# Residual codec kernel on one core: row norms and scores from 64-row blocks on two column tiles, the tap sum kept in z, and the schedule retuned

## The chip, the cores and the metric

The kernel runs on one core of one Trainium2 chip. The metric is the device time of one execution in microseconds (us). Each ratio to the kernel before compares fast runs of one chip session. Two other runs that are compared may come from different sessions, on different chips; the kernel before had a median of 781.0 to 781.5 us in all of them, and where the times and the ratios give different sizes, both are said. The program is static: a small planner inside the kernel's source lays out, before anything runs, in which order each engine issues its instructions and which of two engines gets each shareable piece of work.

## The reference, cut to what matters

```
B, T, D, K = 2, 16000, 512, 3          # Nq, C = 4, 8
z = sum over 3 taps of x[t-1..t+1] * dw_enc          # depthwise
z = z * sigmoid(z)                                   # the gate
res = z; q = 0
for s in range(4):                                   # four codebooks of 8 vectors
    d2  = |res|^2 - 2 res.cb[s] + |cb[s]|^2
    sel = cb[s][argmin(d2)]
    q += sel; res -= sel
y = sum over 3 taps of q[t-1..t+1] * dw_dec
```

All arrays are bfloat16, and the choices have to follow the reference's rounding, so the row norm |res|^2 is needed, once for the first three codebooks and once again for the fourth, from the residual.

Of the kernel before, what the change touches and what calls it, by code (L numbers as in the profile page):

```python
# [16 lines left out]
class Plan:  # L17



    AGAIN = {"PE": 0.0, "ACT": 0.1, "DVE": 0.12, "POOL": 0.1, "SP": 0.0}
# [3 lines left out]
    def __init__(self, pairs, share, quota, when):  # L25
        self.steps, self.writer, self.readers = [], {}, {}
        self.pairs, self.share, self.quota, self.when = pairs, share, quota, when

    def add(self, engine, cost, key, fn, reads=(), writes=(), take=None, free=None, hold=None, tail=0.0, after=(), dest=None):
        n = len(self.steps)  # L30
        deps = set(after)
        for t in reads:
            if t in self.writer:
                deps.add(self.writer[t])
            self.readers.setdefault(t, []).append(n)
        for t in writes:
            if t in self.writer:
                deps.add(self.writer[t])
            deps.update(self.readers.get(t, ()))
            self.writer[t] = n  # L40
            self.readers[t] = []
        deps.discard(n)
        self.steps.append({"n": n, "e": engine, "c": cost, "k": key, "fn": fn, "deps": sorted(deps), "take": take, "free": free,
                           "hold": hold, "tail": tail, "dest": dest})
        return n

    def order(self):
# [3 lines left out]
        rank = [self.when[s["k"][0]][0] + s["k"][1] + self.when[s["k"][0]][1] * s["k"][2] for s in steps]  # L51
# [12 lines left out]

        def place(kind, t):
# [4 lines left out]
        def soonest(s, now):  # L70
            t = max(at[s["n"]], now)
            if s["take"]:
                if s["dest"] == "ANY":
                    if all(held[d] >= self.quota[d] for d in self.quota):
                        return inf
                elif s["dest"] and held[s["dest"]] >= self.quota[s["dest"]]:
                    return inf
                t = place(s["take"][0], t)[0]
            return t

        def open_(n):
            if steps[n]["e"]:
                waiting[steps[n]["e"]].append(n)
# [4 lines left out]
        while len(out) < len(steps):  # L88
            t, _, n = min((soonest(steps[n], clock[e]), rank[n], n) for e, names in waiting.items() for n in names)
            assert t < inf  # L90
            s = steps[n]
            e, c = s["e"], s["c"]
            if s["take"]:
                kind, box = s["take"]
                j = place(kind, t)[2]
# [3 lines left out]
                box["dest"] = s["dest"]  # L99
                if s["dest"] == "ANY":  # L100
                    load = {d: max(clock[d] - t, 0.0) + held[d] + sum(steps[m]["c"] for m in waiting[d] if at[m] <= t + 1.0) for d in ("ACT", "DVE")}
                    full = [d for d in load if held[d] >= self.quota[d]]
                    box["dest"] = ("ACT" if full[0] == "DVE" else "DVE") if full else "DVE" if load["DVE"] + self.share[box["part"]] < load["ACT"] else "ACT"
                    c = c[box["dest"]]
                    steps[n + 1]["e"], steps[n + 1]["c"] = box["dest"], steps[n + 1]["c"][box["dest"]]
                if box["dest"]:
                    held[box["dest"]] += 1
# [3 lines left out]
            s["t"], s["d"] = t, c  # L111
# [8 lines left out]
            waiting[e].remove(n)  # L120
            out.append(s)
            for u in users[n]:
                at[u] = max(at[u], t + c + self.AGAIN[e] if steps[u]["e"] == e else end + self.LATENCY[e])
# [8 lines left out]
def kernel(  # L132
# [21 lines left out]
    ZW = P + NC  # L154
    NX, NP, NZ, NOH, NY = 2, 3, 3, 4, 4
    NA = 4
    SHARE = (6.05, 4.21, -1.54)
    QUOTA = {"ACT": 2, "DVE": 4}
    WHEN = {"setup": (0.738, 0), "load": (-2, 1), "pad": (-1.5, 0), "taps": (0.156, 0.45),
            "exp": (-0.071, 0.45), "plus1": (-0.859, 0.482), "recip": (0.56, 0.492), "gate": (0.894, 0.536),  # L160
            "score0": (1.076, 0.045), "decide": (1.235, 0.171), "win0": (2.058, 0), "resid": (1.684, 0.7),
            "score3": (2.362, 0.507), "decide3": (2.6, 0), "win3": (2.763, 0.334), "back": (2.621, 0.723)}
# [11 lines left out]
    for b, sizes in enumerate(SIZES):  # L174
        done = 0
        for g in sizes:
# [4 lines left out]
                          "split": [(q, min(q + 6, g)) for q in range(0, g, 6)]})  # L181
# [12 lines left out]
    MSK = sb([P, 3, ZW], BF16, "MSK")  # L194
# [6 lines left out]
    P0 = [sb([P, 2, GM * P], BF16, f"P0{b}") for b in range(NP)]  # L201
    P1 = [sb([P, 2, GM * P], BF16, f"P1{b}") for b in range(NP)]
    ZB = [sb([P, KT, GM, ZW], BF16, f"ZB{b}") for b in range(NZ)]
# [21 lines left out]
    plan = Plan(NA, SHARE, QUOTA, WHEN)  # L225
# [36 lines left out]
    def setup():  # L262
# [7 lines left out]
        for u in range(3):  # L270
            add("DVE", 0.2, key, lambda u=u: nc.vector.tensor_scalar(out=MSK[:, u, N3:N3 + P], in0=IDENT, scalar1=BIG, scalar2=-BIG,
                op0=ALU.mult, op1=ALU.add), ["I"], ["MSK"])
# [19 lines left out]
        for b in range(NZ):  # L292
            for i in range(KT):
                eng = "ACT" if b == 0 else "DVE"
                f = nc.scalar.copy if b == 0 else nc.vector.tensor_copy
                add(eng, 0.4, ("setup", 0.9 + b, 0), lambda b=b, i=i, f=f: f(ZB[b][:, i, :, 0:N3], CBM2[:, i:i + 1, 0:N3].to_broadcast([P, GM, N3])),
                    [("CBM2", i)], [("ZC", b)])
                add(eng, 0.25, ("setup", 0.9 + b, 0), lambda b=b, i=i, f=f: f(ZB[b][:, i, :, N3 + P:ZW], CBM2[:, i:i + 1, N3:NC].to_broadcast([P, GM, C])),
                    [("CBM2", i)], [("ZC", b)])
# [99 lines left out]
    def front(st, h):  # L399
# [4 lines left out]
        sl = hc % NP  # L404
        p0, p1 = P0[sl][:, :, 0:R], P1[sl][:, :, 0:R]
        allx = [("X", xs, g) for g in range(1, G + 2)] + [("XE", xs)]
        pt = [[("P0", sl, c) for c in range(2)], [("P1", sl, c) for c in range(2)]]

        def tap(dst, i, k):
            return lambda: nc.vector.tensor_scalar(out=dst, in0=X[:, i, k:k + G, :].rearrange("p g c -> p (g c)"),  # L410
                                                   scalar1=WENC[:, k, i:i + 1], scalar2=None, op0=ALU.mult)
        for k in range(K):
            for c in range(2):
                add("DVE", dve(R, 3.84) + 0.06, ("taps", n, h), tap((p1 if k else p0)[:, c], 2 * h + c, k), allx + ["WENC"], [pt[k > 0][c]])
            if k:
                tt(p0, p0, p1, ALU.add, dve(2 * R, 1.92), ("taps", n, h), pt[1], pt[0])
        add("ACT", act(2 * R), ("exp", n, h), lambda: nc.scalar.activation(p1, p0, ACT.Exp, scale=-1.0),  # L417
            [("P0", sl, 0), ("P0", sl, 1)], [("P1", sl, 0), ("P1", sl, 1), "ACTTAB"], hold="E")
        add("DVE", dve(2 * R, 3.84), ("plus1", n, h), lambda: nc.vector.tensor_scalar(out=p1, in0=p1, scalar1=1.0, scalar2=None, op0=ALU.add),
            [], [("P1", sl, 0), ("P1", sl, 1)])  # L420
        return sl, p0, p1

    def front2(st, h, sl, p0, p1):
        n, G = st["n"], st["G"]
        R = G * P
        add("ACT", act(2 * R), ("recip", n, h), lambda: recip(p1, p1), [], [("P1", sl, 0), ("P1", sl, 1), "ACTTAB"], hold="R")
        Z = ZB[n % NZ]
        o = Z[:, 2 * h:2 * h + 2, 0:G, N3:N3 + P]
        tt(o, p0.rearrange("p i (g c) -> p i g c", c=P), p1.rearrange("p i (g c) -> p i g c", c=P), ALU.mult, dve(2 * R, 1.92),
           ("gate", n, h), [("P0", sl, 0), ("P0", sl, 1), ("P1", sl, 0), ("P1", sl, 1)],  # L430
           [("Z", n % NZ, i, u) for i in (2 * h, 2 * h + 1) for u in range(2)])

# [6 lines left out]
    def gram(st, g0, g1, c0, c1, box):  # L439
        Z = ZB[st["n"] % NZ]  # L440
        w = c1 - c0
        pgr = ps(box)
        for b0 in range(g0, g1, 3):
            nb = min(3, g1 - b0)
            o = pgr[:, 512 * ((b0 - g0) // 3):512 * ((b0 - g0) // 3) + nb * w]
            nc.tensor.matmul(o, lhsT=IDENT, rhs=MSK[:, 0:nb, c0:c1], start=True, stop=False)  # L446
            for u in range(nb):
                for i in range(KT):
                    nc.tensor.matmul(o[:, u * w:(u + 1) * w], lhsT=Z[:, i, b0 + u, N3:N3 + P],  # L449
                                     rhs=Z[:, i, b0 + u, c0:c1], start=False, stop=(u == nb - 1 and i == KT - 1))  # L450

    def views(g0, g1, w, box):
        pgr = ps(box)
        if g1 - g0 == 6:
            return [(g0, 6, pgr.rearrange("p (b w) -> p b w", b=2)[:, :, 0:3 * w].rearrange("p b (u w) -> p b u w", w=w))]
        return [(b0, min(3, g1 - b0), pgr[:, 512 * ((b0 - g0) // 3):512 * ((b0 - g0) // 3) + min(3, g1 - b0) * w].rearrange(
            "p (b u w) -> p b u w", b=1, w=w)) for b0 in range(g0, g1, 3)]

    def grp(t, g0, n):
        return t[:, g0:g0 + n, :].rearrange("p (b u) c -> p b u c", b=2 if n == 6 else 1)  # L460

    def gram_cost(g0, g1, w):
# [258 lines left out]
```

## The kernel before: the parts that the change touches

Rows are handled in 18 tiles; 14 of them hold 16 groups of 128 rows, the first two and the last two hold 6 or 8. The 512 channels are four chunks of 128 partitions (`KT = 4`). One tile passes through these stages.

*Front* (VectorE and ScalarE), in two halves `h` of two channel chunks each. The taps are multiplied and added into `P0`, ScalarE takes `exp` into `P1` and later the reciprocal, and VectorE multiplies the two into z (`ZB`, three buffers). z is first written here, at the gate:

```python
# front: p0, p1 are one of three slots each
for k in range(K):
    for c in range(2):
        add("DVE", ..., tap((p1 if k else p0)[:, c], 2 * h + c, k), ...)
    if k:
        tt(p0, p0, p1, ALU.add, ...)
add("ACT", ..., lambda: nc.scalar.activation(p1, p0, ACT.Exp, scale=-1.0), ...)
add("DVE", ..., p1 = p1 + 1)
# front2
add("ACT", ..., lambda: recip(p1, p1), ...)
o = Z[:, 2 * h:2 * h + 2, 0:G, N3:N3 + P]
tt(o, p0..., p1..., ALU.mult, ..., writes=[("Z", n % NZ, i, u) ...])
```

*Scores* (TensorE, then VectorE). Beside each 128-row block of z lie the codebooks' columns times -2, so one matmul of the block with itself gives the scores and, on the diagonal, the row norms. A mask matmul first puts -2^100 off the diagonal, and VectorE reads the norm as a maximum over the 128 columns:

```python
for u in range(nb):                       # blocks of 128 rows
    for i in range(KT):
        nc.tensor.matmul(o[:, u * w:(u + 1) * w], lhsT=Z[:, i, b0 + u, N3:N3 + P],
                         rhs=Z[:, i, b0 + u, c0:c1], start=False, stop=...)
# ... VectorE:
nc.vector.tensor_reduce(out=rr, in_=v[:, :, :, N3:N3 + P], axis=AX.X, op=ALU.max)
nc.vector.tensor_tensor(out=S, in0=v[:, :, :, 0:N3], in1=CC2, op=ALU.add)
```

*Residual*. TensorE multiplies the one-hot choices with the codebooks, and the 24 results a tile are taken out of PSUM, the memory that TensorE writes its results to, into z. Each of these **evictions** goes either to ScalarE (TensorE then adds z through an identity matmul and ScalarE copies) or to VectorE (which adds). The planner decides for each:

```python
box["dest"] = ... "DVE" if load["DVE"] + self.share[box["part"]] < load["ACT"] else "ACT"
```

After that come the last scores (the same matmuls for the fourth codebook), after which z's buffer is free, and the back stage, which ScalarE copies out for the stores.

## Time and profile before

| | before |
|---|---|
| median of all 4 runs beside the kernel after | 781.2 us |
| span of the profiled run | 779.5 us |
| VectorE (DVE) busy | 729.4 us, 94% |
| ScalarE (ACT) busy | 659.0 us, 85% |
| TensorE (PE) busy | 605.5 us, 78% |
| evictions on ScalarE / on VectorE | 307 / 125 |

These are the first lines of the page of the kernel before: busy time of each engine with its share of the span and its number of instructions, and the busy tenths of VectorE and ScalarE in 40 slices of the span.

```profile
span 779.5 us, 12128 instructions
...
PE 605.5 (78%) x4537; PEld 341.2 (44%) x4537; DVE 729.4 (94%) x1397; ACT 659.0 (85%) x571; POOL 125.4 (16%) x199
...
DVE  8989999999999999999999999999999998679982
ACT  4565977899989999999999999998999987867362
```

VectorE is full from the first slices to the last few. ScalarE is half idle in the first four slices and again at the end; in between both are nearly full.

The next lines are groups of instructions of the kernel before. The columns are line, engine, operation, what is written from what, the count, then busy us and the mean ns of one, then the idle time before them and what ended it. They are the evictions on ScalarE and on VectorE, the score matmuls, and the two diagonal reductions.

```profile
L591 ACT CAST ZB<-ps 128x1024 bf16<-128x1024 f32 (+2 forms) x307 | 276.9, 993 | 67.2 <-PE ps L585 50.8 <-DVE M L620 10.0 <-DVE S L486 5.8
...
L449 PE MATMUL ps<-ZB 128*128 128x152 bf16 (+1 forms) x2016 | 161.7, 232 | 21.2 <-DVE ZB L260 20.0 <-DVE ZB L593 0.9
...
L593 DVE TENSOR_TENSOR ZB<-ZB,ps 128x1024 bf16<-128x1024 bf16 (+2 forms) x125 | 124.0, 1016 | 12.2 <-PE ps L585 6.9 <-ACT ZB L591 4.5 <-ACT YB L652 0.2
...
L610 DVE TENSOR_REDUCE rr<-ps 128x6 bf16<-128x768 f32 (+3 forms) x62 | 43.2, 697 | 2.8 <-PE ps L449 2.6 <-PE ps L534 0.2
L485 DVE TENSOR_REDUCE rr<-ps 128x6 f32<-128x768 f32 (+3 forms) x62 | 43.0, 694 | 5.0 <-PE ps L449 5.0
```

The two reductions together cost VectorE 86.2 us. The same view by shape gives the time of each size: 952 ns for 768 elements of a partition, 553 for 384, 284 for 128.

```profile
L485 DVE TENSOR_REDUCE rr<-ps 128x6 f32<-128x768 f32 x32 | 30.5, 952 | 5.0 <-PE ps L449 5.0
...
L485 DVE TENSOR_REDUCE rr<-ps 128x3 f32<-128x384 f32 x14 | 7.7, 553 | 0.0
...
L485 DVE TENSOR_REDUCE rr<-ps 128x1 f32<-128x128 f32 x14 | 4.0, 284 | 0.0
```

A steady stretch shows what bounds the middle. I mark each tile by the start of its first reduction of the last scores, read from the timeline. Tiles 6 to 11 (counting from 0) of the kernel before span 358.9 to 574.8 us, so five tiles take 215.9 us, **43.2 us a tile**. The windows view of that stretch has, after its length, the busy us and the count for PE, PEld (weight loads), DVE, ACT and POOL, then the granted clock and the share and rate of the DMAs.

```profile
core 0: us, PE busy (x) PEld busy (x) DVE busy (x) ACT busy (x) POOL busy (x), PEclk, DMA share, GB/s
358.90:574.80 215.90, 185.57 (x1437) 104.91 (x1436) 212.12 (x366) 208.84 (x166) 31.02 (x51) 0.98 0.42 96
```

VectorE is busy for 212.1 of 215.9 us (98%), ScalarE for 208.8 (97%).

ScalarE's waits in the kernel before (who waited for whom: us in total, times, the longest) put 25.7 us down to exp waiting for a tap sum, none of it in this steady stretch.

```profile
ACT ZB L591 <- PE ps L585: 50.8, 42, 7.5
ACT P L417 <- DVE P L260: 25.7, 6, 7.8
```

TensorE's pace in the score matmuls is read from its timeline (start, us, engine, operation, count). Twelve of 152 columns and the mask matmul ahead of the next group take 0.99 us.

```profile
305.01 0.95 PE L449 MATMUL ps<-ZB 128*128 128x152 bf16 x12
305.81 0.36 PE L446 MATMUL ps<-MSK,IDENT 128*128 128x456 bf16 x1
306.00 0.95 PE L449 MATMUL ps<-ZB 128*128 128x152 bf16 x12
```

### The profile page before, as it was taken

How to read it: one execution, taken by the hardware profiler on the slowest of the kernel's cores; microseconds unless marked ns; L12 is line 12 of the kernel's file. 1: busy time of each engine (PE TensorE's matmuls, PEld its weight loads, DVE VectorE, ACT ScalarE, POOL GpSimd, SP SyncE). 2: the span in 40 equal slices, each digit the busy share in tenths (PEclk: the TensorE clock that was granted, in tenths of full speed). 3: DMA queues.
4: the chain of work that ended last, by engine and by line, in shares of the span. 5: the costliest groups of instructions: out<-in, count | busy, mean ns of one | idle time of the engine just before them, and what ended most of it. 6: DMA issues, size and time to landing. Idle time of an engine off the chain costs nothing. (4 is left out here: it accounts for less than half of the span.)

```text
span 779.5 us, 12128 instructions
## 1 busy us (share of the span) xinstructions
PE 605.5 (78%) x4537; PEld 341.2 (44%) x4537; DVE 729.4 (94%) x1397; ACT 659.0 (85%) x571; POOL 125.4 (16%) x199
## 2 busy tenths in 40 slices
PE   1154476778869988697978889788979888989884
PEld 0132154355454635336353545445353636454541
DVE  8989999999999999999999999999999998679982
ACT  4565977899989999999999999998999987867362
POOL 2001102223202332020111111010211110111021
PEclk9998696989988999899999999999999999999997
DMA  5442534324342625144361715352422211112032
GB/s 113 99 102 42 127 56 115 68 48 96 120 90 67 139 72 136 28 134 84 108 110 60 151 37 147 61 142 49 120 44 82 68 55 55 55 55 81 28 108 89
DMA packets 148002, 67.03 MB, mean 86 GB/s; under 512 B 139776, under 2 KB 139808, under 8 KB 147944
## 3 DMA queue, kind: packets, MB, share of 16 engines
q1 hardware_dynamic: 137088, 33.06, 21.5%
q0 software_dynamic: 10640, 32.78, 12.9%
q8 instruction: 35, 0.57, 0.3%
q10 hardware_dynamic: 216, 0.43, 0.2%
q14 instruction: 23, 0.19, 0.1%
HBM read 0.43 MB, written 32.77 MB: 43 GB/s over the span
## 5 line engine op out<-in xcount | busy, mean ns | idle before, releaser
L591 ACT CAST ZB<-ps 128x1024 bf16<-128x1024 f32 (+2 forms) x307 | 276.9, 993 | 67.2 <-PE ps L585 50.8
L585 PE MATMUL ps<-OHW,CBN 128*128 128x512 bf16 (+1 forms) x768 | 275.7, 387 | 16.5 <-DVE OHW L561 7.4
L584 PE MATMUL ps<-ZB,IDENT 128*128 128x512 bf16 (+1 forms) x560 | 215.8, 385 | 28.4 <-DVE ZB L593 10.4
L449 PE MATMUL ps<-ZB 128*128 128x152 bf16 (+1 forms) x2016 | 161.7, 232 | 21.2 <-DVE ZB L260 20.0
L449 PEld LDWEIGHTS <-ZB 128*128 128x128 bf16 x2016 | 144.3, 101 | 61.3 <-DVE ZB L260 23.3
L260 DVE TENSOR_TENSOR P<-P,P 128x4096 bf16<-128x4096 bf16 (+2 forms) x72 | 147.7, 2051 | 0.2
L652 ACT CAST YB<-ps 128x1024 bf16<-128x1024 f32 x126 | 132.7, 1077 | 14.3 <-PE ps L644 13.0
L675 POOL DMA_DIRECT2D out_dram<-YB x130 | 76.8, 595 | 416.1 <-ACT YB L652 407.8
L410 DVE TENSOR_SCALAR P<-XT,WENC 128x2048 bf16<-128x2048 bf16 (+2 forms) x216 | 142.4, 686 | 0.2 <-DMA XT<-in_x_dram 0.2
L417 ACT ACTIVATE P<-P 128x4096 bf16<-128x4096 bf16 (+2 forms) x36 | 116.0, 3221 | 25.9 <-DVE P L260 25.7
L585 PEld LDWEIGHTS <-CBN 128*128 128x128 bf16 x768 | 75.8, 99 | 141.2 <-issue 73.6
L593 DVE TENSOR_TENSOR ZB<-ZB,ps 128x1024 bf16<-128x1024 bf16 (+2 forms) x125 | 124.0, 1016 | 12.2 <-PE ps L585 6.9
L435 ACT ACTIVATE P<-P 128x4096 bf16<-128x4096 bf16 (+2 forms) x36 | 113.5, 3186 | 0.2
L644 PE MATMUL ps<-WDEC,OHW 128*128 128x512 bf16 x252 | 81.8, 412 | 11.8 <-DVE OHW L561 6.5
L584 PEld LDWEIGHTS <-IDENT 128*128 128x128 bf16 x560 | 55.3, 99 | 73.6 <-issue 15.3
L446 PE MATMUL ps<-MSK,IDENT 128*128 128x408 bf16 (+4 forms) x188 | 63.3, 336 | 18.8 <-DVE S L486 8.7
L260 DVE TENSOR_TENSOR ZB<-P,P 128x4096 bf16<-128x4096 bf16 (+2 forms) x36 | 72.7, 2019 | 1.5 <-ACT P L435 1.3
L557 PE MATMUL ps<-IDENT,OHA 128*32 128x128 bf16 x504 | 25.2, 238 | 32.5 <-DVE OHA L260 27.2
L644 PEld LDWEIGHTS <-OHW 128*128 128x128 bf16 x252 | 25.8, 103 | 51.4 <-issue 20.2
L485 DVE TENSOR_REDUCE rr<-ps 128x6 f32<-128x768 f32 (+3 forms) x62 | 43.0, 694 | 5.0 <-PE ps L449 5.0
L610 DVE TENSOR_REDUCE rr<-ps 128x6 bf16<-128x768 f32 (+3 forms) x62 | 43.2, 697 | 2.8 <-PE ps L449 2.6
L394 POOL COPY XT<-XT 128x508 bf16<-128x508 bf16 x18 | 14.9, 827 | 185.4 <-DMA XT<-in_x_dram 147.0
(92 smaller groups left out, 438.9 us busy)
## 6 DMA issues: line engine op xcount, KB each, us to landing
out_dram<-YB POOLq DMA_DIRECT2D x33, 448.0 KB, 3.4
out_dram<-YB POOLq DMA_DIRECT2D x28, 512.0 KB, 3.4
XT<-in_x_dram SPq DMA_TRANSPOSE x252, 2.8
out_dram<-YB POOLq DMA_DIRECT2D x30, 60.0 KB, 3.2
out_dram<-YB POOLq DMA_DIRECT2D x31, 2.0 KB, 2.8
out_dram<-YB POOLq DMA_DIRECT2D x2, 224.0 KB, 2.9
YB<-in_dw_dec_dram ACTq DMA_DIRECT2D x1, 384.0 KB, 3.8
out_dram<-YB POOLq DMA_DIRECT2D x1, 384.0 KB, 3.1
```

The source lines that it names most:

```text
L260: add("DVE", cost, key, lambda: nc.vector.tensor_tensor(out=out, in0=a, in1=b, op=op), reads, writes, **kw)
L410: return lambda: nc.vector.tensor_scalar(out=dst, in0=X[:, i, k:k + G, :].rearrange("p g c -> p (g c)"), scalar1=WENC[:, k, i:i + 1], scal ...
L417: add("ACT", act(2 * R), ("exp", n, h), lambda: nc.scalar.activation(p1, p0, ACT.Exp, scale=-1.0), [("P0", sl, 0), ("P0", sl, 1)], [("P1", ...
L435: nc.scalar.add_instruction(mybir.InstActivation(name=nc.get_next_instruction_name(), engine=mybir.EngineType.Activation, func=ACT.Reciprocal,
L449: nc.tensor.matmul(o[:, u * w:(u + 1) * w], lhsT=Z[:, i, b0 + u, N3:N3 + P], rhs=Z[:, i, b0 + u, c0:c1], start=False, stop=(u == nb - 1 an ...
L584: nc.tensor.matmul(o, lhsT=IDENT, rhs=zg[:, k0:k0 + nk, :], start=True, stop=False)
L585: nc.tensor.matmul(o, lhsT=CBN[s, u][:, i * P:(i + 1) * P], rhs=W[:, k0:k0 + nk, PADC:PADC + P], start=not on_act, stop=True)
L591: nc.scalar.copy(zg, v)
L593: nc.vector.tensor_tensor(out=zg, in0=zg, in1=v, op=ALU.add)
L644: nc.tensor.matmul(o, lhsT=W[:, k, PADC:PADC + P], rhs=WDEC[u], start=True, stop=not wrap)
L652: add("ACT", act(1024), key, lambda k=k, box=box, Y=Y, k0=k0: nc.scalar.copy(Y[:, 2 * (k - k0):2 * (k - k0) + 2, :].rearrange("p g d -> p ...
L675: nc.gpsimd.dma_start(out=view[p0:p1, lo:hi, :], in_=Y[p0:p1, lo - g0:hi - g0, :])
```

## The change

The intent is to halve what the diagonal reductions read. Blocks of 64 rows have a 64-column diagonal. Two of them lie side by side on the two halves of the array's columns and write PSUM partitions 0 to 63 and 64 to 127. The codebooks' columns (now all 32) lie beside each 64-row block, so z grows from 160 columns a 128-row group to 192. To make room, the front keeps its sum in z itself: the last tap addition writes z, exp reads z, and the gate multiplies z in place. The front then needs one pair of tap buffers and three exp buffers in place of three `P0` and three `P1`. The planner also gets separate weights for the start, middle and end of the run, and new values.

```diff
-        for k in range(K):  ...
-            if k:
-                tt(p0, p0, p1, ALU.add, ...)
-        add("ACT", ..., lambda: nc.scalar.activation(p1, p0, ACT.Exp, scale=-1.0), ...)
+        for k in range(K):  ...
+            if k == 1:
+                tt(ta, ta, tb, ALU.add, ...)
+        tt(Z, v(ta), v(tb), ALU.add, ..., zt)                 # zt: z's tokens, so z must be free here
+        add("ACT", ..., lambda: nc.scalar.activation(v(ex), Z, ACT.Exp, scale=-1.0), zt, [("EX", sl), ...])
 ...
-        tt(o, p0..., p1..., ALU.mult, ..., [z tokens])
+        tt(Z, Z, v(ex), ALU.mult, ..., [("EX", sl)], zt)
 ...
-                    nc.tensor.matmul(o[:, u * w:(u + 1) * w], lhsT=Z[:, i, b0 + u, N3:N3 + P],
-                                     rhs=Z[:, i, b0 + u, c0:c1], ...)
+                    for h in range(2):
+                        blk = Z[:, i, 2 * (g0 + nb * q + u) + h, :]
+                        nc.tensor.matmul(o[HB * h:HB * h + HB, u * w:(u + 1) * w], lhsT=blk[:, NC:ZW], rhs=blk[:, c0:ZW], ...)
 ...
-    NX, NP, NZ, NOH, NY = 2, 3, 3, 4, 4
+    NX, NE, NZ, NOH, NY = 2, 3, 3, 4, 4
-    SHARE = (6.05, 4.21, -1.54)
-    QUOTA = {"ACT": 2, "DVE": 4}
+    SHARE = (10.17, 2.94, -0.28)
+    QUOTA = {"ACT": 2, "DVE": 2}
 ... (the planner reads its weights by part of the run; new weights WHEN; blocks are read out
      eight groups at a time, not six; the constant columns are filled by ScalarE alone)
```

## The prediction

> **What bounds it now.** The page's busy table has VectorE at 729.4 us and ScalarE at 659.0 us of a 779.5 us span, TensorE at 605.5. The windows view shows both saturated between 150 and 650 us: VectorE about 98%, ScalarE about 96%, TensorE about 85%. Work can be exchanged there: the 432 residual evictions go either to ScalarE (307, 1088 ns for 1024 columns) or to VectorE (125, 1217 ns). So the middle is bound by the *sum* of the two engines over two. In the first 150 us VectorE is full and ScalarE partly idle; in the last 130 us neither is full and the chain of waits runs through score matmuls, VectorE reductions and decisions. VectorE's own waits are small (5.0 + 2.6 us for score matmuls).
>
> **What is removed (groups by shape).** The diagonal reductions read 128 columns a row block: 43.0 + 43.2 us; a reduction of 768 takes 954 ns, 384 takes 556, 128 takes 288, so about 155 ns + 1.04 ns per element. With 64-row blocks half the columns remain, in 8-group pieces: 512 elements, estimated at 687 ns. A 16-group tile then pays 2 x 687 instead of 2752 ns per pass. The score copies (S: 999 ns a tile) become 2 x 192 elements, about 700; the fourth codebook's copies 740 become about 435. Together 7.24 to 3.88 us a 16-group tile, 3.4 us saved; about 52 us in all. Moving the constant-column fill to ScalarE takes some 4 us more off VectorE and puts about 10 us on ScalarE, at the start where it has room.
>
> **What only moves.** The last tap sum written into z and the gate in place keep their number and size: strided output already cost nothing (2285 ns against 2321 contiguous). Exp reads z in 64-element runs; I expect the same 3651 ns. Two exp buffers instead of three should suffice.
>
> **TensorE.** Score matmuls double from 2016 to 4032, at 96 and 72 columns instead of 152 and 136. Today one takes about 66 and 59 ns start to start (12 in 0.80 us in the timeline). The Trainium skill, "TensorEngine Tiling (Array Packing)", Key Properties, says that different tiles can load weights and multiply in parallel, but its Restrictions say column tiling disables fast weight load. This trace agrees on the first: 24 transposes of 128 columns on 32-wide column tiles take 0.63 us, about 18 ns apart, a third of 128 columns' time. No run yet shows 64-wide loads. I estimate 50 to 75 ns per pair of halves, so the score time stays about equal (roughly 100 to 150 us against 126), and mask matmuls save about 12 us. TensorE is not the bound either way.
>
> **Sum.** In the middle 3.4 us a tile is shared: moving about 1.5 evictions a tile to VectorE gives about 1.6 us a tile, some 22 us in all. Start and tail, where VectorE is alone on the path, give some 5 us more; the schedule retuned separately for start, middle and end perhaps 5 to 8. Predicted: **747 us**, 8 in 10 between **728 and 766**. Faster by over 2%: 0.89; within 2%: 0.09; slower: 0.02.
>
> **What would show it.** Reductions near 690 ns x32 per pass, both lines near 21 us; VectorE busy near 695 to 705, ScalarE near 640 to 650; VectorE evictions up from 125 to 140 to 160; both still above 95% in the middle; score pairs below 80 ns; exp and gate times unchanged.
>
> **What would make it wrong.** Unpacked or slow weight loads (over 100 ns a pair) would make evictions wait for TensorE; 64-element runs could slow 2-byte VectorE or ScalarE work; z held from the tap sum on, or two exp buffers, could stall the front; a lower granted clock from a less busy array; or retuning could gain more than I allow.

## The result, and the profile after

The kernel after takes 756.66 us (median of 4 runs, 755.21 to 757.46) against 781.2. The ratio is 0.9687, with a 95% interval of 0.9661 to 0.9713, so it is 3.1% faster. Ratios here and below are the mean time of one kernel's fast runs over that of the other's of the same rounds, so they are not quite the ratio of the medians quoted.

The same lines of the page, of the kernel after:

```profile
span 754.4 us, 15788 instructions
...
PE 549.0 (73%) x6425; PEld 281.0 (37%) x6425; DVE 719.4 (95%) x1286; ACT 640.0 (85%) x549; POOL 131.8 (17%) x199
...
DVE  8989999999999999999999999999999999989992
ACT  7776897939799698998989899898989899988575
```

TensorE and ScalarE fell; VectorE fell by 10.0 us only, although some 56 us of work had been taken off it by the prediction's sum. In the middle ScalarE's row now has 8s among the 9s. The groups that answer to those of before:

```profile
L626 ACT CAST ZB<-ps 128x1024 bf16<-128x1024 f32 (+2 forms) x281 | 236.2, 918 | 35.0 <-PE ps L620 32.6 <-ACT ZB L626 0.7 <-DVE rr L521 0.7
...
L628 DVE TENSOR_TENSOR ZB<-ZB,ps 128x1024 bf16<-128x1024 bf16 (+2 forms) x151 | 162.7, 1098 | 5.1 <-PE ps L620 5.0
...
L486 PE MATMUL ps<-ZB 128*64 128x96 bf16 (+1 forms) x4032 | 106.7, 210 | 21.3 <-DVE ZB L298 21.1 <-ACT ZB L626 0.2
...
L521 DVE TENSOR_REDUCE rr<-ps 128x8 f32<-128x512 f32 (+1 forms) x32 | 21.6, 674 | 2.7 <-PE ps L486 2.7
L645 DVE TENSOR_REDUCE rr<-ps 128x8 bf16<-128x512 f32 (+1 forms) x32 | 21.5, 673 | 4.1 <-PE ps L486 4.1
```

The reductions are as forecast, 21.6 and 21.5 us. (Their means of 674 and 673 ns mix two shapes; by shape, those of 512 elements take 682 and 681 ns.) But VectorE now does 151 evictions, and more of the full-sized ones: their busy time rose from 124.0 to 162.7 us. Here is the steady stretch, again tiles 6 to 11, now 335.6 to 552.0 us.

```profile
core 0: us, PE busy (x) PEld busy (x) DVE busy (x) ACT busy (x) POOL busy (x), PEclk, DMA share, GB/s
335.60:552.00 216.40, 170.55 (x2027) 87.21 (x2027) 214.61 (x342) 196.17 (x151) 42.02 (x49) 0.96 0.37 98
```

This is the main finding. **Five tiles take 216.4 us, 43.3 us a tile, as before.** (Over seven tiles, 6 to 13, it is 42.7 us a tile before and 43.3 after; one expectation below uses that 42.7.) VectorE is at 99%, ScalarE at 91%. Counting evictions on VectorE in the two stretches gives 25 before (30.4 us) and 40 after (48.0 us). So eight evictions a tile instead of five: 17.5 us more, against the 5 x 3.4 = 17 us that the new scores save. The middle's saving was spent on evictions that ScalarE did before.

Where the 25.1 us of span came from, by the same marks:

| | before | after | difference |
|---|---|---|---|
| to the mark of tile 6 | 358.9 us | 335.6 us | -23.3 |
| tiles 6 to 11 | 215.9 | 216.4 | +0.5 |
| from the mark of tile 11 to the end | 204.7 | 202.4 | -2.3 |

The first row is not all saved work. Up to that mark VectorE's idle time is the same in both kernels, 11.5 and 11.3 us, so the 23.3 us are work that VectorE has not done by then, although it has done 45 evictions instead of 30. Part of it is the saved score work, and part is only put off. By the mark of tile 6 the kernel before had done 126 tap multiplications, the kernel after 113, which is one tile's front (12) less. So the kernel after runs a shallower pipeline, which fills sooner and leaves that front for later, where VectorE had been idle: from the mark of tile 11 on its idle time falls from 34.9 to 21.9 us. VectorE's idle time over the whole span (span less busy) fell from 50.1 to 35.0 us. In this sum the 25.1 us are 10.0 us less busy and 15.1 us less idle.

Why is ScalarE short of work? These are its waits in the kernel after.

```profile
ACT L455 <- DVE ZB L298: 37.0, 11, 11.9
ACT ZB L626 <- PE ps L620: 32.6, 47, 5.0
...
ACT EX L455 <- DVE ZB L298: 11.7, 5, 5.8
```

The load of the exp table and exp itself now wait 48.7 us for VectorE's writes of z, against 25.7 us before; 13.5 us of that lies in the five steady tiles, once a tile and 2.7 us each:

```profile
ACT L455 <- DVE ZB L298: 13.5, 5, 2.7
```

That is about the 12.7 us by which ScalarE's busy time in the stretch fell (208.8 to 196.2). The longest such wait, before the steady stretch, in ScalarE's and then in VectorE's and TensorE's timelines:

```profile
155.18 1.94 ACT L626 CAST ZB<-ps 128x1024 bf16<-128x1024 f32 x2
169.00 1.28 ACT L455 ACT_TABLE_LOAD   x1 [11.88 <-DVE ZB L298]
```

```profile
131.71 2.28 DVE L298 TENSOR_TENSOR ZB<-TA,TB 128x4096 bf16<-128x4096 bf16 x1
...
164.11 0.68 DVE L645 TENSOR_REDUCE rr<-ps 128x8 bf16<-128x512 f32 x1
...
166.63 2.28 DVE L298 TENSOR_TENSOR ZB<-TA,TB 128x4096 bf16<-128x4096 bf16 x1
```

```profile
162.86 0.71 PE L486 MATMUL ps<-ZB 128*64 128x72 bf16 x32
```

ScalarE had nothing to do from 157.1 us until the tap sum that begins at 166.63 was done. That sum is the eleventh, the first half of tile 5, and goes into the same z buffer as tile 2. Tile 2's last score matmuls read that buffer until 163.6 us, and their reduction is the one at 164.11. The previous tap sum had been at 131.71. Before, the sum went to its own buffer, and only the gate, with two ScalarE passes in between, waited for z.

TensorE's score matmuls in the timeline, at full clock:

```profile
331.92 0.71 PE L486 MATMUL ps<-ZB 128*64 128x72 bf16 x32
...
340.50 0.87 PE L486 MATMUL ps<-ZB 128*64 128x96 bf16 x32
```

With 0.20 us from the start of one to its end, 32 of them start (0.87 - 0.20) / 31 = 22 ns apart for 96 columns and 16 ns for 72. A pair costs 43 and 33 ns, against 66 and 59 ns for one full-width matmul before.

### The profile page after: what moved, and what is told of

Read it like the earlier page. It is cut to its first block, busy times and chain, and to the rows that moved or that the text cites. A ratio compares the mean times of both kernels' runs of the same rounds, so it can differ in the third digit from the quotient of the medians.

```text
span 754.4 us, 15788 instructions
## 1 busy us (share of the span) xinstructions
PE 549.0 (73%) x6425; PEld 281.0 (37%) x6425; DVE 719.4 (95%) x1286; ACT 640.0 (85%) x549; POOL 131.8 (17%) x199
## 3 DMA queue, kind: packets, MB, share of 16 engines
q0 software_dynamic: 10640, 32.78, 12.7%
## 5 line engine op out<-in xcount | busy, mean ns | idle before, releaser
L626 ACT CAST ZB<-ps 128x1024 bf16<-128x1024 f32 (+2 forms) x281 | 236.2, 918 | 35.0 <-PE ps L620 32.6
L628 DVE TENSOR_TENSOR ZB<-ZB,ps 128x1024 bf16<-128x1024 bf16 (+2 forms) x151 | 162.7, 1098 | 5.1 <-PE ps L620 5.0
L455 ACT ACTIVATE EX<-ZB 128x4096 bf16<-128x4096 bf16 (+2 forms) x36 | 115.5, 3209 | 12.8 <-DVE ZB L298 11.7
L486 PE MATMUL ps<-ZB 128*64 128x96 bf16 (+1 forms) x4032 | 106.7, 210 | 21.3 <-DVE ZB L298 21.1
L486 PEld LDWEIGHTS <-ZB 128*64 128x64 bf16 x4032 | 90.0, 116 | 71.1 <-issue 42.1
L467 ACT ACTIVATE EX<-EX 128x4096 bf16<-128x4096 bf16 (+2 forms) x36 | 115.0, 3198 | 0.2
L446 DVE TENSOR_SCALAR TB<-XT,WENC 128x2048 bf16<-128x2048 bf16 (+2 forms) x144 | 95.1, 678 | 0.0
L298 DVE TENSOR_TENSOR ZB<-ZB,EX 128x4096 bf16<-128x4096 bf16 (+2 forms) x36 | 72.6, 2016 | 1.1 <-ACT EX L467 1.0
L298 DVE TENSOR_TENSOR TA<-TA,TB 128x4096 bf16<-128x4096 bf16 (+2 forms) x36 | 72.9, 2024 | 0.1
L298 DVE TENSOR_TENSOR ZB<-TA,TB 128x4096 bf16<-128x4096 bf16 (+2 forms) x36 | 72.5, 2014 | 0.0
L446 DVE TENSOR_SCALAR TA<-XT,WENC 128x2048 bf16<-128x2048 bf16 (+2 forms) x72 | 51.8, 728 | 0.4 <-issue 0.2
```

Source lines behind the costliest of these rows:

```text
L298: add("DVE", cost, key, lambda: nc.vector.tensor_tensor(out=out, in0=a, in1=b, op=op), reads, writes, **kw)
L446: return lambda: nc.vector.tensor_scalar(out=dst, in0=X[:, i, k:k + G, :].rearrange("p g c -> p (g c)"), scalar1=WENC[:, k, i:i + 1], scal ...
L455: add("ACT", act(2 * R), ("exp", n, h), lambda: nc.scalar.activation(v(ex), Z, ACT.Exp, scale=-1.0), zt, [("EX", sl), "ACTTAB"], hold="E")
L467: nc.scalar.add_instruction(mybir.InstActivation(name=nc.get_next_instruction_name(), engine=mybir.EngineType.Activation, func=ACT.Reciprocal,
L486: nc.tensor.matmul(o[HB * h:HB * h + HB, u * w:(u + 1) * w], lhsT=blk[:, NC:ZW], rhs=blk[:, c0:ZW], start=False, stop=(u == nb - 1 and i = ...
L626: nc.scalar.copy(zg, v)
```

## Experiments

Theory **H** after the comparison: z is now claimed at the tap sum, earlier than at the gate, and this delays the fronts. ScalarE runs dry, the planner has to hand evictions to VectorE, and so the middle gains nothing. The rivals were that TensorE's many small matmuls slow the middle; that retuning, not the new blocks, made the gain; that no order could have filled ScalarE better; and that the shared tap buffers, not the hold of z, are to blame.

"Weights" below are the planner's tuning values. For several kernels I searched them with the planner alone (random changes, kept mostly when the planned span fell; 13 minutes for before_retuned, 40 for the others, for scores_alone and scores_act after a shorter search). No time here comes from the planner: each is a run.

| run | ratio to before | us | us a tile, 6 to 11 | ScalarE busy there | evictions on VectorE there |
|---|---|---|---|---|---|
| before | 1 | 781 | 43.2 | 97% | 25 |
| after | 0.9687 | 756.7 | 43.3 | 91% | 40 |
| b_half_reduce (wrong) | 0.969 | 755.3 | 41.5 | 99.9% | 25 |
| a_half_reduce (wrong) | 0.9485 | 739.0 | 42.3 | 92% | 40 |
| a_unpaired | 0.9719 | 757.7 | 43.3 | 91% | 40 |
| front_only | 1.0874 | 847.7 | 50.5 | 75% | 46 |
| before_retuned | 0.9959 | 778.2 | 43.4 | 97% | 25 |
| scores_alone | 0.9464 | 739.1 | 41.8 | 96% | 35 |
| scores_act | 0.9651 | 753.4 | 42.6 | 98% | 25 |
| after_old_weights | 1.0326 | 806.3 | 46.1 | 83% | 43 |
| hold_only | 1.0244 | 799.9 | 48.1 | 77% | 55 |
| hold_retuned | 0.964 | 753.3 | 43.0 | 90% | 42 |
| front_retuned | 0.9903 | 774.2 | 44.5 | 91% | 34 |
| scores_best | 0.9466 | 739.5 | 41.7 | 96% | 34 |

All are correct except the two that are wrong. Percentages and counts are of each run's own stretch from the mark of tile 6 to that of tile 11.

### b_half_reduce: relieve VectorE and change nothing else

```diff
 # the kernel before
-  tensor_reduce(out=rr,  in_=v[:, :, :, N3:N3 + P], ...)      # 128 columns
+  tensor_reduce(out=rr,  in_=v[:, :, :, N3:N3 + P // 2], ...) # 64: wrong norms for half the rows
-  tensor_reduce(out=rr3, in_=v[:, :, :, 0:P], ...)
+  tensor_reduce(out=rr3, in_=v[:, :, :, 0:P // 2], ...)
```

> The kernel before with its diagonal reductions reading only the first half of each block's columns (a wrong result on purpose); every instruction, its order and its engine stay the same. VectorE loses about 33 us of work (768 columns 954 ns to 384 columns 556, and so on). Theory S (before, VectorE and ScalarE bound the middle together, so relief of one alone is mostly wasted until work is exchanged): 765 us, no more than about half of the 33 us comes back. Rival V (VectorE alone is the path): about 750 us, nearly all of it comes back.

Measured: 755.3 us; the instruction order on every engine is unchanged. The reductions fell from 86.2 to 52.1 us, so 34.1 us of relief gave 25.7 us by the medians and some 24 by the ratio, 70 to 75%. My "no more than half" was wrong, and so was its picture of the middle as the sum of two engines over two. Without any exchange the middle went from 43.2 to 41.5 us a tile, and there ScalarE became the full engine:

```profile
core 0: us, PE busy (x) PEld busy (x) DVE busy (x) ACT busy (x) POOL busy (x), PEclk, DMA share, GB/s
347.90:555.20 207.30, 182.02 (x1427) 103.58 (x1436) 201.90 (x367) 207.08 (x166) 37.18 (x51) 1.00 0.43 100
```

ScalarE is busy for 207.08 of 207.30 us. So the kernel before was bound by VectorE with ScalarE close behind. And 34 us off VectorE, with the order untouched, did as much as the whole change did with some 56.

### a_half_reduce: the same relief in the kernel after

```diff
 # the kernel after
-  tensor_reduce(out=rr,  in_=v[:, :, :, NC:ZW], ...)            # 64 columns
+  tensor_reduce(out=rr,  in_=v[:, :, :, NC:NC + HB // 2], ...)  # 32: wrong on purpose
 # and likewise for rr3
```

> The kernel after with its diagonal reductions reading 32 instead of 64 columns of each block (a wrong result on purpose), same order and engines. VectorE loses 60 reductions x about 0.26 us, some 16 us. Theory: in the kernel after VectorE alone bounds the middle (99% against ScalarE's 88%), so nearly all comes back: 756.7 to about 742 us. Rival (still both): half of it, about 749 us.

Measured: 739.0 us. The reductions fell by 17.0 us and the time by 17.7, or by 15.8 by the ratios. All of it, or nearly all, came back: in the kernel after VectorE is the path.

### a_unpaired: the order of the two column tiles

```diff
-                for i in range(KT):
-                    for h in range(2):
+                for h in range(2):
+                    for i in range(KT):
```

> The kernel after with its score matmuls ordered four of one half, then four of the other, instead of alternating the two column tiles; the same work and results. If the two halves overlap because they alternate, a pair costs more[...], about 100 to 190 ns, and score matmuls take 50 to 200 us more of TensorE. Theory (TensorE is not the bound): the time rises by less than 1.5%. Rival (TensorE's pace matters as much as VectorE's): it rises by over 3%.

Measured: 757.7 us, as the kernel after within its spread, and the score matmuls hardly slower:

```profile
303.18 0.90 PE L486 MATMUL ps<-ZB 128*64 128x96 bf16 x32
```

32 matmuls take 0.90 us, not 0.87. A pair now takes 45 ns, not 43. The expected 100 ns a pair did not appear: the two halves need not alternate matmul by matmul to overlap. Because their cost did not rise, this run does not test how much TensorE's pace matters. That TensorE is not the bound rests on its 79% in the steady stretch and on a_half_reduce.

### front_only: the front's change alone, weights and blocks of before

```diff
 # the kernel before, with the newer planner at the old weights
-  if k: tt(p0, p0, p1, ALU.add, ...)
+  if k == 1: tt(ta, ta, tb, ALU.add, ...)
+  tt(Z, v(ta), v(tb), ALU.add, ..., zt);  exp: ex <- Z;  gate: Z = Z * ex
```

> The kernel before, 128-row blocks and its own schedule weights and split, with only the front of the change: the last tap sum written to z, exp from z, gate in place. It needs the same instructions, but z is taken from the tap sum on, not from the gate. Theory H (the early hold of z delays the front and has to be bought back by retuning): slower than before by 3 to 7%, 805 to 835 us, with ScalarE waiting for the tap sum. Rival (the front's change is free): within 1% of 781 us.

Measured: 847.7 us, 8.7% slower, worse than expected. ScalarE waits 138.5 us for tap sums, against 25.7:

```profile
ACT L453 <- DVE ZB L292: 106.3, 12, 12.9
...
ACT EX L453 <- DVE ZB L292: 32.2, 8, 9.7
```

The front's change is not free, though its instructions cost the same. The newer planner is not part of this: at the old weights it builds the kernel before as the same program, instruction for instruction (checked by building both; nothing was run for it). But the old weights were tuned for another dependency, so part of this is disorder; the retuned runs below separate that.

### before_retuned: the newer planner and searched weights on the old kernel

```diff
 # the kernel before; only the planner class and its weights differ
-  WHEN = {"taps": (0.156, 0.45), ...}
+  WHEN = {"taps": three pairs, one each for start, middle and end, ...}   # searched
```

> The kernel before, same instructions and buffers, but with the newer planner that has separate weights for start, middle and end, and weights searched for it. Question: how much of the 24 us is retuning alone. Theory (the start's gain is VectorE work removed, not retuning): at most 8 us faster than before, about 773 us, and tile 6 starts its last scores within 2 us of the kernel before. Rival (retuning by parts is the gain): 755 to 765 us, with the gain in the first seven tiles.

Measured: 778.2 us, 0.4% below before, with tile 6 at 358.4 us against 358.9. Retuning alone, at least as far as my search got, is not where the gain came from.

### scores_alone: the new blocks with the old front

```diff
 # the kernel after
-  TA, TB, three EX; the tap sum in z
+  three P0, three P1 as before; z is written at the gate
-  NY = 4
+  NY = 3; the set-up tables CB1, CB4, SEL and ROW lie in the third z buffer until it is filled
   # weights searched anew
```

Without such savings it does not fit: the plain combination needs 214.3 KB a partition and 207.9 are left. Moving the sum into z is the change's way to make it fit.

> 64-row blocks and column tiles, but the front of the kernel before (tap sum in its own buffer, z taken only at the gate); room for it is made by three instead of four output buffers and by laying set-up tables in z. Weights searched anew for it. Theory H (in the kernel after the early hold of z keeps ScalarE short of work, so VectorE takes evictions and the middle gains nothing): the middle period falls below the 43.2 us a tile that before and after share, to about 41.5, ScalarE's waits for tap sums fall from 49 us to under 30, time 740 to 748 us. Rival (the middle cannot be filled better whatever the front): period 43, time 755 us or more.

Measured: 739.1 us, ratio 0.9464, correct: 17.5 us below the kernel after, and the fastest structure here that gives right results. It is a little better than the range that I gave. The steady stretch and the wait for tap sums over the whole run:

```profile
core 0: us, PE busy (x) PEld busy (x) DVE busy (x) ACT busy (x) POOL busy (x), PEclk, DMA share, GB/s
333.90:542.70 208.80, 169.09 (x2035) 86.43 (x2036) 208.19 (x337) 200.93 (x156) 41.52 (x50) 0.98 0.50 102
```

```profile
ACT P L464 <- DVE P L308: 15.5, 11, 4.0
```

208.8 us for five tiles is 41.8 us a tile. ScalarE is at 96%, VectorE at 99.7% with seven evictions a tile. The wait for tap sums fell from 48.7 to 15.5 us. By the planner's own times, a search of 40 minutes on the kernel after itself found no better weights; no run tested that, and hold_retuned below is the test on the chip. So the middle can be filled better when z is not held early, and the saving that I forecast for it (1.6 us a tile) appears: 43.2 - 41.8 = 1.4.

### scores_act: the same kernel, more evictions on ScalarE

```diff
 # scores_alone with other searched weights: 319 evictions on ScalarE instead of 290
```

> The same kernel as scores_alone with other searched weights that leave far more evictions with ScalarE (319 of 432, against 290 there and 281 in the kernel after). If VectorE and ScalarE can be traded freely without the early hold, the middle period stays near 42.3 us and ScalarE is busy above 95% of the middle; if ScalarE starves in any case, it stays near 88% and the period exceeds 43. Time about 755 us, as its tail is poorly ordered.

Measured: 753.4 us. In the middle ScalarE is at 98%, VectorE at 95% with five evictions a tile, and the period is 42.6 us. So without the hold ScalarE can be kept full. This split is past the best one, and its tail is poor, as expected.

### after_old_weights: the whole change at the old weights

```diff
 # the kernel after
-  SHARE, QUOTA, WHEN of the kernel after
+  SHARE, QUOTA, WHEN of the kernel before
```

> The whole change, but with the weights, split offsets and quota of the kernel before. Theory H: the old order assumes that fronts run ahead of z, so this is slower than before in spite of 56 us less VectorE work: 805 to 820 us. Rival (retuning is a refinement): about 760 us, faster than before.

Measured: 806.3 us, 3.3% slower than before. The retuning in the change is no refinement: without it the change loses.

### hold_only: one dependency added to scores_alone

```diff
-                tt(p0, p0, p1, ALU.add, ..., pt[1], pt[0])
+                tt(p0, p0, p1, ALU.add, ..., pt[1], pt[0] + (zt if k == K - 1 else []))
```

> The kernel scores_alone with one more dependency and nothing else: the last tap addition also waits until z's buffer is free, as it does in the kernel after. Same instructions and buffers, same weights; the planner lays the order anew around the extra wait. Theory H: this alone brings back what the kernel after shows: ScalarE waits for tap sums of over 40 us, ScalarE below 92% of its middle, evictions moved to VectorE, a period of 44 us or more, 785 to 805 us. Rival (shared tap buffers or in-place gate are to blame): within 1% of scores_alone's 739.

Measured: 799.9 us. Instructions and buffers are those of scores_alone; only the last tap addition must also wait for z. ScalarE waits 61.6 us for tap sums, and 55 evictions of the five steady tiles go to VectorE:

```profile
ACT P L465 <- DVE P L308: 61.6, 18, 15.5
```

The in-place gate and the shared tap buffers are absent here, so they are not what it takes to bring the effect about. Disorder from untuned weights is again a part of it.

### hold_retuned: the same, with weights searched as long

```diff
 # hold_only with searched weights
```

> hold_only with weights searched for it as long as for scores_alone. Theory H: retuning buys back the disorder but not the hold: near the kernel after, 755 to 765 us, a period near 43 us. Rival (only missing tuning, no cost of the hold): 740 to 745 us, a period near 41.5.

Measured: 753.3 us, near the kernel after (756.7), though a little below the range that I gave.

```profile
339.90:555.00 215.10, 172.06 (x1974) 86.59 (x1975) 213.66 (x343) 194.32 (x148) 29.14 (x49) 0.92 0.54 97
```

215.1 us for five tiles is 43.0 us a tile, VectorE at 99%, ScalarE at 90%, 42 evictions on VectorE: the totals of the kernel after. Over the whole run ScalarE waits 41.2 us for tap sums, against 15.5 without the hold. But inside the steady stretch it hardly waits for them; there it waits for TensorE's matmuls of the back stage:

```profile
ACT YB L702 <- PE ps L694: 16.7, 11, 3.6
ACT P L465 <- DVE P L308: 2.7, 4, 1.1
```

So the searched order moved the wait, and ScalarE stays short of work all the same. Why these matmuls come late was not tested, so the chain from the hold to the idle ScalarE is seen in the kernel after and in hold_only, but not in this middle. Retuning buys back the disorder (799.9 to 753.3), not the hold. Against scores_alone, one added dependency costs 753.3 - 739.1 = 14 us after tuning on both sides. In the profiled spans (752.6 against 737.5 us) 6.0 us of it come before the mark of tile 6, 6.3 in the five steady tiles and the rest after.

### front_retuned: the front's change alone, with searched weights

```diff
 # front_only with searched weights
```

> front_only (128-row blocks, z taken at the tap sum) with weights searched for it as long. Theory H: the period stays 1 to 2 us above the kernel before's 42.7, about 44.5; a better start may make up for part of it; 772 to 785 us in all. Rival (the hold costs nothing once tuned): the period returns to 42.7 or less.

Measured: 774.2 us, 1% below before, which is clear of the noise. The middle is worse, 44.5 us a tile, as the theory says. But tile 6 is reached at 336.9 us, 22 us sooner than before, with no score work saved. So the early hold is not only a loss: with fitting weights it comes with a start that is nearly as quick as that of the kernel after. Part of that is work put off: 112 tap multiplications are done by that mark, against 126 before, and from the mark of tile 11 to the end it takes 213.0 us, against 204.7. On 128-row blocks gain and loss about cancel. Nor does a quick start need the hold: scores_alone reaches the mark at 334.0 us.

### scores_best: a longer search

```diff
 # scores_alone with weights from a second search
```

> scores_alone with weights from a second, longer search. Theory: the split is near what it can be; about 738 us, within 0.5% of scores_alone, period 41.3.

Measured: 739.5 us, the same as scores_alone. Within this planner and my search, about 739 us is what the new blocks are worth with the old front.

## Why the prediction was right or wrong

The time was inside the range (728 to 766) and the direction right, at 756.7 us against 747. The sum behind it was only partly right: the gain of the middle did not come, and a start that gained more than was forecast made up for much of it. That the two met near 747 is luck.

- **Work removed from VectorE: right.** Reductions of 512 elements were forecast at 687 ns and 21 us a pass; they take 682 and 681 ns, 21.6 and 21.5 us.
- **TensorE: right direction, cheaper than estimated.** A pair costs 43 or 33 ns at full clock, below the 50 to 75 estimated. TensorE's busy time fell by 56.5 us, and it is not the bound. The Trainium skill, "TensorEngine Tiling (Array Packing)", Key Properties, says that tiles work in parallel, and the trace agrees: one after the other, two halves of 96 columns would take an estimated 83 ns at the 0.43 ns a column of the kernel before (66 ns for 152), and a pair takes 43. The loss of fast weight load that its Restrictions name is not visible as a limit here: each of these matmuls has its own load of 64 columns. The profile records such a load at 116 ns on average, and one of 128 columns at 101 ns before, so a load is not shorter, but it does not set the pace.
- **Exp, gate: right.** Exp takes 3640 ns from 64-element runs (3651 before), the in-place gate 2283 (2285 before).
- **"In the middle 3.4 us a tile is shared ... about 1.6 us a tile, some 22 us in all": this step failed.** The middle gained nothing (43.2 to 43.3 us a tile), and "both still above 95%" failed with it: ScalarE is at 91%. The saving went into three more evictions a tile on VectorE, while ScalarE waits for tap sums. ScalarE's wait for tap sums, 13.5 us there, is about all that its busy time fell by. The cause is the part of the change that I counted as "only moves": z is claimed at the tap sum. The prediction named "z held from the tap sum on" as a risk but gave it no time. The runs give it a size: 14 us on these blocks after tuning (hold_retuned against scores_alone), and the forecast period does appear without it (41.8).
- **"Start and tail ... some 5 us more", retuning "5 to 8": too small.** 23.3 us came before the mark of tile 6. That made up for the missing middle, so the total came out close by luck. How the start's gain divides is in part open. Saved work mostly returns there when the order is kept (b_half_reduce takes 13.3 us of reductions away by that mark and gains 11.0 us), and the front's change with searched weights, which does fewer fronts by that mark, gives 22 us in front_retuned. Retuning of the old kernel gave 0.5 us there.
- **VectorE busy 695 to 705: missed at 719.4**, and for the same reason. Its evictions rose to 151 (140 to 160 forecast), but more of them are the full-sized ones (123 of 1024 columns against 83), so their time rose by 38.7 us; 26 more evictions at 1.2 us would have been 31. ScalarE at 640.0 was within its forecast.
- **"Two exp buffers instead of three" was a misreading of the diff.** The change keeps three; no run tested two.
- **"The middle is bound by the sum of the two engines over two" was too simple.** With the order kept, 70 to 75% of VectorE's relief in the kernel before came back, until ScalarE was full.

What the runs show is that the hold alone brings the stalled middle back. What they do not show is by which waits it does so in every order (hold_retuned's middle has others than the kernel after), nor a best order: all tuned comparisons rest on searches of limited length. I could not try the kernel after with a fourth z buffer; it needs 24 KB more a partition, and about 206 of the 207.9 KB are taken (the 214.3 of the plain combination less the 8 of one front buffer).

## What to carry to other kernels

When a change makes a buffer's life start earlier, count that as a cost even if every instruction keeps its duration: list what must finish before the first write now, and which engine waits for that write. Check a forecast saving stage by stage with a mark per tile, because a total can agree while the stage that was to pay gains nothing and another makes up for it. And when two engines share work, look at the work that changed hands before calling a saving lost.

## What the Trainium skill lacked or had wrong

- "TensorEngine Tiling (Array Packing)", Performance Considerations: it has no time for two 64-wide column tiles with a new weight load for each matmul. Here a pair took 43 ns for 96 columns and 33 ns for 72 at full clock, start to start within a bank, where one full-width matmul took 66 ns for 152 columns and 59 for 136.
- "TensorE: Matmul & The Clock Gate", Part 1 ("Wait — 56ns, not 53.3ns?"), says that start-to-start never drops below about 25 ns however few the columns, and does not say that this is meant for one tile of the array. On alternating column tiles the trace shows 16 ns (32 matmuls of 72 columns in 0.71 us, the last one's 0.20 us taken off), or 33 ns from one matmul to the next on the same tile. So there is no such floor over the two column tiles together, at least as this profile places the starts, and nothing here speaks against one within a tile. What is missing is the scope: Part 3 of the same page itself has packed tiles starting about 4 ns apart.
- Neither page says whether the two tiles must alternate in the order of issue. Four matmuls of one half and then four of the other took 0.90 us for 32, against 0.87 us alternating.
